# Other distances for the loads, splits, turns and swaps of q, k and v in a fused attention and feed-forward kernel

## The chip, the cores and the metric

The kernel runs on one core of a Trainium2 chip. The metric is the device time of one execution in microseconds (us), and lower is better. The engines are called by their short names: PE (TensorE, matmuls), ACT (ScalarE), DVE (VectorE), POOL (GpSimd) and SP (SyncE, which issues most of the DMAs here).

## The reference

Attention runs over 8 batches and 8 heads, with 576 rows of 64 numbers each for q, k and v. Scores under the row's maximum less tau (0.02) are cut off before the softmax. The heads are put side by side to rows of 512, and two matrix products with a shrinking function between them follow.

```python
scores = scale * np.matmul(q, k.transpose(0, 1, 3, 2))
thresh = np.max(scores, axis=-1, keepdims=True) - tau
scores = np.where(scores >= thresh, scores, -1000000000.0)
attn = np.exp(scores - np.max(scores, axis=-1, keepdims=True))
attn = attn / (np.sum(attn, axis=-1, keepdims=True) + 1e-09)
x = np.matmul(attn, v)            # then (b, h, s, d) -> (b * s, h * d)
h = x @ w_in                      # 4608 x 512 by 512 x 2048
out = (h - np.tanh(h)) @ w_out    # 2048 x 512
```

## The kernel before

**Pairs, tiles and slots.** Two heads of one batch make a pair; there are 32 pairs (`NPAIR`), four to a batch. A pair's scores are cut into nine tiles of 128 query rows by 576 keys: four for each head and a ninth of the 64 remaining rows of both. A main loop over `s` is the schedule, written out by hand (the tile framework runs in its manual order). One value of `s` is called a slot here, and one score tile belongs to each. In slot `s` the loop emits the scores of tile `s + 8` (`AHEAD`), the cut-off of tile `s + 5` (`MASK`), the exp of tile `s` and the product with v of a tile two slots back (`LAG`). Every engine's instructions stand in the order in which the loop emits them.

**One tile's way.** `scores(i)` runs the products on PE in fp16: q and k are each split into a high and a low half of fp16 which lie side by side on the 128 partitions, so the product with `kT` and the one with `kS` (k with its two halves swapped) are summed (L401 for the ninth tile, L410 for the others). DVE scales the tile and takes its maximum (L420). ACT applies the cut-off (`kink`, L447, writes z). For the first six pairs PE turns z; from pair 6 on SP issues a DMA transpose for every second tile, which takes two tiles at once (L454, zT from z). ACT then applies the exp (`weights`, L483, writes pT), and PE multiplies with v (`attend`, L506, L513, L524). That transpose is issued five slots ahead of the exp that reads it. Counted from the slot of a pair's first scores, these transposes lie at even distances (2, 4, 6, 8, 10) for an even pair, and zT(-10) stands for the one ten slots before that slot.

**Preparing a pair.** Six kinds of step make q, k and v ready. A load brings them from memory in up to two parts: `load_part` (L175) is issued by ACT's queue, and the steps are named `k0`, `q0`, `q1`, `v0` and `v1`. `split` (`ks`, `qs`: L228, L231, L232, three POOL instructions) makes the fp16 halves, khl or qhl. `turn` (`kt`, `qt`: L315) is a DMA transpose on SP's queue for q from pair 8 and for k from pair 9; before that PE turns them. `swap` (`kw`: L337, two POOL copies) makes kS from kT. `split_v` (`vs`: L261, L265, L266) casts v on POOL. The raw tiles and the halves have two buffers each, kT, kS and qT three, v four.

**Where these steps stand.** For pairs 8 and up the tables `LATER` (by even and odd pair) and `FIRST_LATER` (pairs 8 and 9) give each step a distance in slots. A step with distance `d` goes to the slot `9p - 8 - d`, which is `d` slots before the slot of the pair's first scores, and is emitted at the end of that slot, behind the scores, cut-offs, exps and products. So a step of distance 9 follows zT(-10) and precedes zT(-8) in SP's queue. [...]POOL's splits, casts and swaps of an even pair and of the odd pair after it are one queue, and SP's zT transposes, turns and stores of the output are another.

**The rest of PE's work.** Between the attention steps the loop emits the two products of the feed-forward part for an earlier batch: `hidden` (L579, psH), then tanh on ACT (`bend`, L592) and the difference on DVE (`shrink`, L598, writes g), then `project` (L605, psY). After the last attention tile these run alone.

Of the kernel before, what the change touches and what calls it, by code (L numbers as in the profile page):

```python
# [18 lines left out]
def kernel(  # L19
# [713 lines left out]
    def w_load(piece):  # L733
# [6 lines left out]
        else:  # L740
# [18 lines left out]

    LATER = {  # L760
        0: (
            ("kt", 11), ("qt", 7), ("k0", 18), ("q0", 17), ("v0", 13),
            ("q1", 14), ("v1", 10), ("ks", 12), ("qs", 8), ("vs", 4),
            ("kw", 6),
        ),
        1: (
            ("kt", 10), ("qt", 6), ("k0", 18), ("q0", 14), ("v0", 15),
            ("q1", 13), ("v1", 12), ("ks", 11), ("qs", 8), ("vs", 6),
            ("kw", 5),
        ),  # L770
    }
# [4 lines left out]
            ("kw", 3),  # L776
        ),
        9: (
            ("kt", 10), ("qt", 6), ("k0", 18), ("q0", 14), ("v0", 15),
            ("q1", 13), ("v1", 12), ("ks", 11), ("qs", 8), ("vs", 6),  # L780
            ("kw", 5),
        ),
    }
# [177 lines left out]
```

## Time and profile before

| what | us |
|---|---|
| median of 3 runs | 507.79 |
| lowest and highest run | 505.07, 510.07 |
| profiled execution, its own time | 511.62 |
| its span, first to last instruction | 509.7 |
| PE busy | 484.8 |
| ACT busy | 431.7 |
| DVE busy | 400.2 |
| POOL busy | 291.4 |

The profile is of one execution. Its span is 1.9 us less than that execution's own time, and this execution took 3.8 us more than the median of the runs. A row of the timeline has the start, the length, the engine (SPq and ACTq are the DMA issues of SP and ACT), the line of the kernel, the operation, and what is written from what (out<-in). A row of the waits has who waited for what, the sum in us, how many times, and the longest.

### The profile page before, as it was taken

What the parts mean: (1) busy time and instruction counts of PE and PEld (TensorE: products, weight loads), DVE (VectorE), ACT (ScalarE), POOL (GpSimd) and SP (SyncE); (2) the same over time, 40 slices, a digit from 0 to 9 for tenths busy, and PEclk for the clock granted to TensorE, in tenths of its full rate; (3) what the DMA queues carried; (4) which work ended last, traced back from release to release, by engine and by line L of the source; (5) the groups of instructions that cost most, each with busy time, mean ns of one, the idle gap of its engine ahead of it and who ended that gap; (6) DMA issues with size and microseconds to landing.
All of it is one profiled execution on the core that took longest, in us unless ns stands there. A gap on an engine that the chain in (4) does not pass through costs nothing.

```text
span 509.7 us, 12184 instructions
## 1 busy us (share of the span) xinstructions
PE 484.8 (95%) x4283; PEld 270.9 (53%) x4345; DVE 400.2 (79%) x1150; ACT 431.7 (85%) x617; POOL 291.4 (57%) x390
## 2 busy tenths in 40 slices
PE   8999899889999989999999999999998999999997
PEld 4666566445555545555555555555554555544444
DVE  5899978878889879988898789889886887544440
ACT  5999998889999889999999999899979999533430
POOL 8999999886765375757675666569456700000000
PEclk9999999989999999999999999999999999999999
DMA  7852658999999999999999999999999986311013
GB/s 206 262 155 89 195 190 220 159 225 214 231 217 245 192 254 209 238 241 242 242 195 221 261 238 225 207 242 240 213 191 258 187 144 115 87 41 42 23 41 82
DMA packets 233341, 95.32 MB, mean 187 GB/s; under 512 B 203968, under 2 KB 222656, under 8 KB 233280
## 3 DMA queue, kind: packets, MB, share of 16 engines
q1 hardware_dynamic: 212336, 72.87, 75.1%
q10 hardware_dynamic: 20944, 21.67, 16.1%
q8 instruction: 34, 0.56, 0.5%
q14 instruction: 27, 0.22, 0.2%
HBM read 36.70 MB, written 9.44 MB: 91 GB/s over the span
## 4 chain that ended last, share of the span: by engine, by line
PE 57%; POOL 12%; DMA 9%; issue 7%; ACT 7%; DVE 5%; ACTq 1%; SPq 0%; POOLq 0%; DVEq 0%
PE psY L605 18%; PE psH L579 14%; PE psS L410 13%; DMA zT<-z 6%; PE psO L513 3%; POOL kS L337 3%; PE psHt L579 3%; ACT pT L483 3%; DMA vraw<-in_v_dram 3%; ACT z L447 2%; DVE g L598 2%; POOL qhl L232 2%; DVE sc L420 2%; PE psS L401 2%; ACTq L175 1%
## 5 line engine op out<-in xcount | busy, mean ns | idle before, releaser
L420 DVE TENSOR_SCALAR_CACHE_REDUCE sc<-psS 128x576 f32<-128x576 f32 x288 | 213.5, 752 | 27.1 <-PE psS L410 12.9
L447 ACT ACTIVATE z<-sc,nb 128x576 bf16<-128x576 f32 x288 | 216.1, 770 | 8.0 <-DVE nb L432 5.7
L483 ACT ACTIVATE pT<-zT 128x1152 f16<-128x1152 bf16 x117 | 135.2, 1155 | 12.3 <-DMA zT<-z 10.6
L605 PE MATMUL psY<-w_out_sb,g 128*128 128x512 bf16 (+1 forms) x564 | 140.8, 373 | 1.6 <-issue 0.2
L579 PE MATMUL psH<-xT,w_in_sb 128*128 128x512 bf16 x448 | 119.4, 381 | 5.1 <-issue 2.0
L337 POOL COPY kS<-kT 64x1152 f16<-64x1152 f16 x62 | 70.8, 1142 | 86.3 <-DMA kT<-khl 72.7
L598 DVE SCALAR_TENSOR_TENSOR g<-th,psH 128x512 bf16<-128x512 f32 x128 | 87.6, 685 | 33.6 <-ACT th L592 32.9
L410 PE MATMUL psS<-kT,qT 128*128 128x512 f16 (+1 forms) x512 | 104.7, 286 | 4.1 <-DVE sc L420 1.9
L410 PE MATMUL psS<-kS,qT 128*128 128x512 f16 (+1 forms) x512 | 105.1, 287 | 0.0
L410 PEld LDWEIGHTS <-qT 128*128 128x128 f16 x1024 | 72.5, 98 | 59.0 <-issue 3.8
L592 ACT ACTIVATE th<-psH 128x512 f32<-128x512 f32 x128 | 74.6, 583 | 21.4 <-PE psH L579 21.4
L605 PEld LDWEIGHTS <-g 128*128 128x128 bf16 x592 | 51.1, 98 | 54.6 <-DVE g L598 0.4
L579 PEld LDWEIGHTS <-w_in_sb 128*128 128x128 bf16 x576 | 49.4, 98 | 57.4 <-issue 6.3
L513 PE MATMUL psO<-vb,pT 128*128 128x65 bf16 x1024 | 53.3, 194 | 0.0
L513 PEld LDWEIGHTS <-pT 128*128 128x128 f16 x1024 | 44.2, 98 | 9.6
L232 POOL TENSOR_TENSOR qhl<-qraw,qhl 128x576 f16<-128x576 f32 x31 | 39.7, 1281 | 2.6
L232 POOL TENSOR_TENSOR khl<-kraw,khl 128x576 f16<-128x576 f32 x31 | 39.7, 1280 | 2.7
L475 ACT ACTIVATE pT<-psZ 128x512 f16<-128x512 bf16 (+1 forms) x54 | 35.1, 654 | 2.4 <-PE psZ L466 2.1
L506 PE MATMUL psO<-vb,pT 128*128 128x130 bf16 x128 | 28.2, 220 | 3.7 <-ACT pT L483 3.6
L617 DVE COPY yo<-psY 128x512 f32<-128x512 f32 (+1 forms) x31 | 21.1, 680 | 13.1 <-PE psY L605 12.4
L539 DVE TENSOR_TENSOR osb<-psO,rc 128x256 bf16<-128x256 f32 x64 | 27.2, 424 | 2.2
L228 POOL TENSOR_SCALAR qraw<-qraw 128x576 f32<-128x576 f32 x31 | 20.8, 671 | 11.1 <-DMA qraw<-in_q_dram 10.8
(77 smaller groups left out, 452.1 us busy)
## 6 DMA issues: line engine op xcount, KB each, us to landing
out_dram<-yo SPq DMA_DIRECT2D x32, 256.0 KB, 3.8
kraw<-in_k_dram ACTq DMA_DIRECT2D x24, 288.0 KB, 4.2
qraw<-in_q_dram ACTq DMA_DIRECT2D x24, 256.0 KB, 4.3
wt<-in_moe_w_in_dram SPq DMA_DIRECT2D x8, 512.0 KB, 4.6
wt<-in_moe_w_out_dram SPq DMA_DIRECT2D x8, 512.0 KB, 3.9
vraw<-in_v_dram ACTq DMA_DIRECT2D x24, 160.0 KB, 4.3
vraw<-in_v_dram ACTq DMA_DIRECT2D x24, 128.0 KB, 3.8
vraw<-in_v_dram SPq DMA_DIRECT2D x8, 256.0 KB, 3.6
```

The lines of the kernel that those rows point to most:

```text
L232: nc.gpsimd.tensor_tensor(out=hl[:, :, 1, :], in0=x, in1=hl[:, :, 0, :], op=ALU.subtract)
L337: nc.gpsimd.tensor_copy(out=o, in_=i)
L410: nc.tensor.matmul(out=ps[:, dst], lhsT=lhs, rhs=cols(p, kk, hh), start=(n == 0), stop=(n == 1),)
L420: nc.vector.tensor_scalar(out=sc, in0=ps[:, lo : lo + S], scalar1=SC, scalar2=None, op0=ALU.mult, op1=ALU.max, accum_out=mx[:, c : c + 1],)
L447: nc.scalar.activation(out=z, in_=sc, func=ACT.Prelu, bias=nb, scale=1.0, alpha=STEEP)
L475: nc.scalar.activation(out=pt[:, off * P : (off + n) * P], in_=ps[:, 0 : n * P], func=ACT.Exp)
L483: nc.scalar.activation(out=pt[:, 0 : n * P], in_=zts.pop(i)[:, 0:n, :], func=ACT.Exp)
L513: nc.tensor.matmul(out=po[:, t - 1 + ab, :], lhsT=pt[:, blk * P : (blk + 1) * P], rhs=vb[:, hh, c, :], start=False, stop=(n == 7), skip_gr ...
L579: nc.tensor.matmul(out=ps, lhsT=w_in_sb[:, c, n * P : (n + 1) * P], rhs=xs[m][:, c, :] if m < B else xR[:, c, :, :], start=(c == 0), stop= ...
L592: nc.scalar.activation(out=th, in_=ps, func=ACT.Tanh)
L598: nc.vector.scalar_tensor_tensor(out=gs[m][:, n, :], in0=th, scalar=-1.0, in1=ps, op0=ALU.mult, op1=ALU.add,)
L605: nc.tensor.matmul(out=ps, lhsT=gs[m][:, n, ms * P : (ms + 1) * P], rhs=w_out_sb[:, n, cols], start=(n == 0), stop=(n == DF_C - 1),)
```

## The change

Only numbers in the two tables change, so the same instructions are emitted in another order on ACT's load queue, POOL and SP. For even pairs from 10: the turn of k goes from 11 slots before the scores to 9, the split of q from 8 to 10, the cast of v from 4 to 6, the swap of k from 6 to 3, the second part of q's load from 14 to 15 and that of v's from 10 to 12. For odd pairs from 9: the split of k goes from 11 to 14, the split of q from 8 to 9, the first load of k from 18 to 20, q's two parts from 14 and 13 to 15 and 14, and the first part of v from 15 to 16. Pair 8 keeps its own table. Two neighbours in POOL's queue change places: an even pair's swap of k now follows the next odd pair's split of k and that even pair's own cast of v.

```diff
     LATER = {
         0: (
-            ("kt", 11), ("qt", 7), ("k0", 18), ("q0", 17), ("v0", 13),
-            ("q1", 14), ("v1", 10), ("ks", 12), ("qs", 8), ("vs", 4),
-            ("kw", 6),
+            ("kt", 9), ("qt", 7), ("k0", 18), ("q0", 17), ("v0", 13),
+            ("q1", 15), ("v1", 12), ("ks", 12), ("qs", 10), ("vs", 6),
+            ("kw", 3),
         ),
         1: (
-            ("kt", 10), ("qt", 6), ("k0", 18), ("q0", 14), ("v0", 15),
-            ("q1", 13), ("v1", 12), ("ks", 11), ("qs", 8), ("vs", 6),
+            ("kt", 10), ("qt", 6), ("k0", 20), ("q0", 15), ("v0", 16),
+            ("q1", 14), ("v1", 12), ("ks", 14), ("qs", 9), ("vs", 6),
             ("kw", 5),
         ),
     }
...
         9: (
-            ("kt", 10), ("qt", 6), ("k0", 18), ("q0", 14), ("v0", 15),
-            ("q1", 13), ("v1", 12), ("ks", 11), ("qs", 8), ("vs", 6),
+            ("kt", 10), ("qt", 6), ("k0", 20), ("q0", 15), ("v0", 16),
+            ("q1", 14), ("v1", 12), ("ks", 14), ("qs", 9), ("vs", 6),
             ("kw", 5),
         ),
```

## The prediction, made before the result was known

> **What bounds the kernel now.** I read the stretches first. The six steps that the change moves belong to the pairs whose turns go by DMA, so only the time from 100 us to about 440 us counts; after that the projections run out alone. Columns: length, then busy time of PE, PEld, DVE, ACT and POOL with instruction counts, granted clock, DMA share, GB/s.
>
> ```profile
> 120.00:180.00 60.00, 59.32 (x533) 32.78 (x541) 52.51 (x157) 57.78 (x80) 37.09 (x47) 1.00 1.22 219
> 180.00:200.00 20.00, 18.50 (x155) 9.68 (x155) 15.31 (x46) 18.62 (x26) 14.89 (x20) 1.00 1.12 228
> 200.00:320.00 120.00, 118.49 (x1052) 65.20 (x1069) 106.65 (x315) 116.31 (x160) 78.25 (x100) 1.00 1.19 234
> 320.00:340.00 20.00, 19.14 (x177) 10.72 (x177) 16.48 (x52) 18.21 (x26) 10.24 (x13) 1.00 1.24 216
> 340.00:380.00 40.00, 39.58 (x344) 21.74 (x349) 35.73 (x105) 38.34 (x54) 25.79 (x36) 1.00 1.23 231
> 380.00:400.00 20.00, 17.80 (x157) 9.46 (x158) 15.19 (x46) 17.03 (x24) 13.13 (x17) 1.00 1.19 210
> 400.00:440.00 40.00, 39.00 (x331) 21.31 (x335) 30.92 (x88) 36.62 (x50) 6.00 (x8) 1.00 0.76 141
> ```
>
> PE is idle 20 us x 16 less 311.8 us busy, so 8.2 us in all from 120 to 440 us. [...]a 512-column matmul starts 215 to 216 ns after the one before it nearly everywhere, so the stretch is PE-bound and **8.2 us (1.6%) is all that a schedule can win here**. ACT is almost as full (about 96%). What the waits in the same stretch name:
>
> ```profile
> POOL kS L337 <- DMA kT<-khl: 71.0, 19, 7.9
> ACT pT L483 <- DMA zT<-z: 8.8, 10, 2.2
> ```
>
> POOL waits a lot in `swap` (L337) for the turned k, but POOL has room. ACT's 8.8 us are the waits that reach PE: the exp (L483) waits for its transposed scores, then PE waits for the exp. So what matters is when SP issues each zT transpose[...]. SP's own rows around an even pair's turn:
>
> ```profile
> 275.69 1.49 SPq L454 DMA_TRANSPOSE zT<-z  x1
> 277.67 2.71 SPq L315 DMA_TRANSPOSE kT<-khl  x1
> 280.47 3.42 SPq L454 DMA_TRANSPOSE zT<-z  x2
> 283.99 1.38 SPq L315 DMA_TRANSPOSE qT<-qhl  x1
> ```
>
> SP ends 275.69 + 1.49 = 277.18 and starts the turn at 277.67: 0.49 us idle. Between most neighbours it is 0.10 us, so 0.38 us was a wait. The z that the 280.47 row takes had ended at 277.80; the turn held it back.
>
> [...]a zT row lasts 1.47 us in the median and lands 4.7 us after its start.[...]
>
> **The change part by part.** A slot is one score tile; over the pairs it lasts 1.45 to 1.5 us (a pair of nine is 12.5 to 15 us). No instruction is added or removed.
>
> *Gap between split and turn* (even k 1 to 3 slots, q 1 to 3; odd k 1 to 4, q 2 to 3). What it can remove is SP waiting for POOL. From 110 to 425 us I took every hole before a turn of k over the usual 0.10 us whose end lies 28 ns after a split: 0.16 + 0.38 + 0.23 + 0.50 + 0.04 = **1.3 us over 22 pairs**; q's turn has none. POOL already runs ahead. Only the 0.38 us one reaches an ACT wait. I take 0.4 us of ACT; bounds 0 and 1.3.
>
> *Even turn of k from 11 to 9 slots before the scores.* zT transposes are issued at even distances here, so the turn leaves the place before zT(-10) and comes before zT(-8); q's turn stays at 7, before zT(-6). SP's order becomes zT, kT, zT, qT, zT, where one place of pause lay between. I moved the rows by hand for the even pairs 12 to 30, with each row's own length. zT(-10) is issued 0.2 to 2.6 us earlier; zT(-8) 0 to 1.1 us later; zT(-6) 0 to 0.7 us later, 0.35 us typically. What they have to spare, from landing to the exp that reads it (0.08 us means that the exp was started by it):
> - zT(-10): 0.08 five times of 11, and ACT waited 1.09 + 1.05 + 0.03 us there. Gain: up to 2.2 us of ACT; the 1.09 us is in a stretch where every DMA was slow (zT landings of 7 to 8.8 us from 167 to 177 us), so I take 1.3.
> - zT(-8): 0.08, 0.08, 0.15, 1.03, then more. A delay of 0.35 us costs 1.0 us in the sum over 12.
> - zT(-6): 0.08, 0.08, 0.14, 0.26, 0.42, 0.53, 0.72, 0.74, 0.77, then more. A delay of 0.35 us costs 1.2 us in the sum, 0.7 us costs 3.4, 1.5 us costs 10.6.
>
> So ACT: -0.4 - 1.3 + 1.0 + 1.2 = **+0.5 us**. PE lost 8.2 us while ACT waited 8.8, but about 2 us of PE's are 0.16 us holes after the remainder tiles (L401) of every two pairs, so 6 of 8.8: a factor of 0.7. That is +0.35 us.
>
> *Swap of k, even, from 6 to 3.* Both copies (2 x 1.14 us) are queued on POOL behind v's casts and behind the next odd pair's split of k (0.67 + 0.66 + 1.28 us), which was behind the swap before. Those have their data long before kT lands, so the swap still starts when kT lands. New turn start: zT(-10)'s issue end, about 12.2 us before the pair's first scores, plus a landing of 5.2 us median, 8.8 worst, plus 2.3 us of copies: done 4.7 us ahead in the median, 1.1 us in the worst. It is wanted about 0.7 us ahead (I count from the first score's row on DVE; its matmuls start that much sooner). Cost 0; if a slow DMA stretch meets it, 1 to 2 us once. Behind the swap stands the odd pair's split of q, wanted by SP some 8 us later: no cost.
>
> *Loads earlier* (odd k by 2 slots, q0, q1 and v0 by 1; even q1 by 1, v1 by 2). Same number of issues on ACT, each in a slot of its own. Splits already find their data except 10.8 us of POOL waits on q, which only shorten. The raw buffers are two deep and the split two pairs back is done over ten slots before: no wait for them on ACT. The 160 KB of v and 288 KB of k that stood beside zT(-10) and zT(-8) come two slots sooner, beside zT(-12), which has 1.6 us to spare in the median; v0 and q0 come one slot nearer to qT and zT(-6). The trace can't price this: between -1 and +2 us; I take 0.
>
> *v's casts, even, two slots earlier*: three POOL instructions (0.62 + 0.29 + 0.29 us), read by PE much later. Nothing.
>
> Sum: +0.35 us on the profiled execution, 511.62 us with 509.7 us of span. That execution lies 3.8 us above the median of 507.79, by the slow DMA stretches that account for its stalls at 183 and 382 us, which the change doesn't touch. Against the median: 508.1 us.
>
> **Rivals.**
> - *Faster*: the places before zT(-10) and after an odd turn lose their waits and the earlier loads keep clear of even turns. Of 8.2 us of idle PE, some 2 us are fixed; winning the other 6 gives 501.8, half of it 504.8. For it: ten zT waits, half of them next to turns. Against: the two largest are slow DMA stretches, not POOL.
> - *Slower*: the row of five transposes without a pause. Each holds SP 1.5 us, five need 7.3 us and have 8.8 us of slots; [...]zT(-6) comes 1.5 us late instead of 0.35. Price 10.6 us of ACT waits, times 0.7: +7.4 us, so 515. It decides from a mean delay of about 1.1 us (some 7 us of ACT, 5 us of PE). For it: zT(-6) has the least to spare now. Against: moved by hand, no pair exceeds 0.7 us.
> - *No effect at all*: SP never waited for the splits to begin with, 507.8.
>
> **How the numbers follow.** This kernel's runs spread from 505.07 to 510.07, so 1% (5.1 us) is what a measurement can tell from no change. No effect or nearly, with half a gain or a small loss on either side: 0.60, at 508.1, own range 505 to 511. Slower by over 1%: 0.28, since two tight places lie behind the new bunch, and the swap's cover shrinks from 6 to 3 slots. Faster by over 1%: 0.12, as it needs nearly all idle PE. The range goes to 502.5 and 515.
>
> **What would show it.** Right: zT(-10) issued within 0.5 us of its z in even pairs, spare time there up by a microsecond, zT(-6) down by some 0.3 us; holes before turns of k all 0.10 us; POOL's wait before swaps smaller or the same; idle PE from 120 to 440 us within 6 to 10 us. Wrong: PE rows waiting for kS at the first tile of even pairs (swap too late), ACT waits on zT over 15 us in the sum, or loads that land later than 5 us in the median.

## The result and the profile after

The changed kernel is slower: 513.34 us in the median of 15 runs, 508.38 us for the kernel before in as many, and a ratio of 1.0116 with a 95% interval of 1.009 to 1.0143. Every ratio here is of the fast runs alone (it leaves out runs over 1.5% above the fastest of their kernel), while the medians are over all runs, so a ratio can differ by some tenths of a percent from the quotient of the two medians. The time lies inside the range given (502.5 to 515), 5.2 us above the time forecast (508.1), and the ratio is on the slower side of the 1% line, which had been given 0.28. The profiled execution of after took 519.0 us (span 517.2), the longest of its 15, that of before 511.62 us; so the two traces differ by 7.4 us where the medians differ by 5.0, and sizes read from them are on the large side.

The stretches of after, with the columns as in the prediction (length, then busy PE, PEld, DVE, ACT and POOL with counts, granted clock, DMA share, GB/s; the DMA share adds up the packets' own times, and reaches 1.23 here):

```profile
120.00:180.00 60.00, 56.78 (x502) 31.11 (x510) 49.58 (x150) 54.92 (x76) 37.14 (x47) 1.00 1.23 220
180.00:200.00 20.00, 18.95 (x167) 10.25 (x167) 15.93 (x48) 18.29 (x25) 11.18 (x14) 1.00 1.14 219
200.00:320.00 120.00, 115.79 (x1009) 62.96 (x1025) 101.75 (x301) 111.48 (x153) 75.55 (x97) 0.99 1.23 222
320.00:340.00 20.00, 16.50 (x129) 8.32 (x131) 13.08 (x41) 15.27 (x21) 8.93 (x12) 0.92 1.22 177
340.00:380.00 40.00, 38.65 (x343) 21.21 (x346) 34.48 (x101) 37.87 (x53) 25.95 (x34) 1.00 1.19 231
380.00:400.00 20.00, 19.74 (x182) 11.03 (x184) 17.47 (x53) 19.24 (x27) 15.06 (x21) 1.00 1.20 242
400.00:440.00 40.00, 39.23 (x327) 21.12 (x332) 32.74 (x95) 37.64 (x52) 8.24 (x10) 1.00 0.84 153
```

PE is idle for 320 - 305.6 = 14.4 us there, 8.2 us before. Idle time is not the whole loss in this trace: the granted clock was 0.51 from 234.2 to 237.6 us and from 336.6 to 340.0 us (the 0.92 of the stretch from 320 to 340). Each drop stands close to the end of a wait of PE for the exp, of 2.0 us to 233.2 and of 2.8 us to 336.7. Four matmuls of `project` take 1.90 us in the second and 1.03 at full clock, so each drop costs about 1.7 us (an estimate: half of 3.4). In the trace of before there is one such drop (0.50) ahead of the end, at 104.3 us, outside the stretch. That the waits caused the drops is not shown. The waits of the same stretch of after (who, for what, sum in us, times, longest):

```profile
POOL kS L337 <- DMA kT<-khl: 64.9, 20, 9.8
POOL qraw L228 <- DMA qraw<-in_q_dram: 24.9, 12, 4.3
ACT pT L483 <- DMA zT<-z: 19.6, 19, 3.3
PE psO L506 <- ACT pT L483: 6.5, 4, 2.8
```

ACT's waits for zT went from 8.8 us in 10 to 19.6 us in 19. This is the row that moved with the time: in the 14 profiles of this document it goes from 6.4 us (an execution of 506.36 us) to 20.1 us (518.97 us), and the five executions of over 516 us are the five with over 15 us of it. It moves with the time of the execution that was profiled, though, and not only with the kernel, so a row of one execution can't say by itself which kernel is slow; the ratios do that. POOL's longer waits for q (24.9 us, 10.8 before) and its shorter ones for kT (64.9 us, 71.0 before) don't reach PE: it has no wait for qT or kS in this stretch of after.

### The profile page after: what moved, and what is told of

It is laid out like the page before. It is cut to its first block, busy times and chain, and to the rows that moved or that the text cites. A ratio compares the mean times of both kernels' runs of the same rounds, so it can differ in the third digit from the quotient of the medians.

```text
span 517.2 us, 12173 instructions
## 1 busy us (share of the span) xinstructions
PE 487.9 (94%) x4283; PEld 271.7 (53%) x4345; DVE 399.6 (77%) x1150; ACT 432.4 (84%) x617; POOL 291.7 (56%) x390
## 4 chain that ended last, share of the span: by engine, by line
PE 56%; DMA 11%; ACT 9%; POOL 9%; issue 6%; DVE 6%; ACTq 1%; SPq 0%; POOLq 0%; DVEq 0%
PE psY L605 18%; PE psH L579 14%; PE psS L410 12%; DMA zT<-z 9%; ACT z L447 3%; PE psO L513 3%; ACT pT L483 3%; PE psHt L579 3%; POOL kS L337 2%; PE psS L401 2%; DVE g L598 2%; DVE sc L420 2%; DMA vraw<-in_v_dram 2%; ACT th L592 2%; ACTq L175 1%
## 5 line engine op out<-in xcount | busy, mean ns | idle before, releaser
L483 ACT ACTIVATE pT<-zT 128x1152 f16<-128x1152 bf16 x117 | 135.2, 1156 | 20.3 <-DMA zT<-z 19.6
L605 PE MATMUL psY<-w_out_sb,g 128*128 128x512 bf16 (+1 forms) x564 | 142.3, 376 | 1.6 <-issue 0.2
L337 POOL COPY kS<-kT 64x1152 f16<-64x1152 f16 x62 | 70.9, 1143 | 69.0 <-DMA kT<-khl 64.9
L228 POOL TENSOR_SCALAR qraw<-qraw 128x576 f32<-128x576 f32 x31 | 20.9, 673 | 24.9 <-DMA qraw<-in_q_dram 24.9
```

The source lines that it names most:

```text
L337: nc.gpsimd.tensor_copy(out=o, in_=i)
L483: nc.scalar.activation(out=pt[:, 0 : n * P], in_=zts.pop(i)[:, 0:n, :], func=ACT.Exp)
L605: nc.tensor.matmul(out=ps, lhsT=gs[m][:, n, ms * P : (ms + 1) * P], rhs=w_out_sb[:, n, cols], start=(n == 0), stop=(n == DF_C - 1),)
```

## The experiments

Each kernel differs from the kernel before, or from the changed one, only in distances of the two tables. The ratio is to the kernel before on the same chip, with its 95% interval. Three theories stood at the start. A: the turn of k, now in a row of transposes without a pause, makes the transposes late. B: the earlier loads do it through the DMA engines. C: the new order on POOL does it.

**The turn of k alone.**

```diff
 LATER[0]
-            ("kt", 11),
+            ("kt", 9),
```

> The kernel before with one edit: the even pairs' turn of k at 9 slots before the scores, not 11. Theory A (the turn of k sits in a row of five transposes without a pause, and the transposes behind it come late): 3 to 5 us slower than before, ratio 1.006 to 1.010. Theory B (the earlier loads press on the DMA engines where the transposes have least to spare): within 1 us of before. Theory C (the new order on POOL costs): within 1 us of before.

Measured: 507.95 us, ratio 1.0004 (0.9979 to 1.003). A, in the form of the prediction's slower rival, falls: the turn in its new place costs nothing that can be measured. From the waits of this kernel between 120 and 440 us, in an execution of 506.36 us (reader, what it waits for, sum in us, times, longest):

```profile
ACT pT L483 <- DMA zT<-z: 6.4, 8, 1.7
```

**The loads alone.**

```diff
 LATER[0]
-            ("q1", 14), ("v1", 10)
+            ("q1", 15), ("v1", 12)
 LATER[1], FIRST_LATER[9]
-            ("k0", 18), ("q0", 14), ("v0", 15), ("q1", 13)
+            ("k0", 20), ("q0", 15), ("v0", 16), ("q1", 14)
```

> The kernel before with only the load distances of the change (even q1 15, v1 12; odd k0 20, q0 15, v0 16, q1 14). Theory B: 3 to 5 us slower than before, ratio 1.006 to 1.010. Theories A and C: within 1 us of before.

Measured: 514.49 us, ratio 1.0112 (1.0074 to 1.015). This is as large as the change's whole effect, as theory B says, and a little over the 1.010 that it gave. The same row of this kernel's waits, in an execution of 518.97 us, is as long as that of after:

```profile
ACT pT L483 <- DMA zT<-z: 20.1, 15, 3.4
```

**The change with the old turn of k.**

```diff
 the changed kernel, LATER[0]
-            ("kt", 9),
+            ("kt", 11),
```

> The changed kernel with the even turn of k put back to 11 slots. Theory A: back to the kernel before within 1.5 us. Theories B and C: as slow as the changed kernel, 4 to 6 us over before.

Measured: 517.6 us, ratio 1.0191 (1.014 to 1.0243), on six runs. Putting the turn back doesn't help. The kernel is some 9 us over before, more than the 4 to 6 us that B and C gave: with the earlier loads the old place of the turn is, on these few runs, worse than the new one. No theory had that, and it stays unexplained.

**The change with the old loads.**

```diff
 the changed kernel, LATER[0]
-            ("q1", 15), ("v1", 12)
+            ("q1", 14), ("v1", 10)
 LATER[1], FIRST_LATER[9]
-            ("k0", 20), ("q0", 15), ("v0", 16), ("q1", 14)
+            ("k0", 18), ("q0", 14), ("v0", 15), ("q1", 13)
```

> The changed kernel with all load distances put back. Theory B: back to the kernel before within 1.5 us. Theories A and C: as slow as the changed kernel, 4 to 6 us over before.

Measured: 507.56 us, ratio 0.999 (0.996 to 1.0021). So the splits, casts, swaps and the turn of k together are worth nothing that can be measured with the old loads, and C falls too. The row in this kernel (an execution of 506.08 us) is that of before again:

```profile
ACT pT L483 <- DMA zT<-z: 8.4, 10, 2.0
```

**Which load?** B was divided: into a run of three loads in adjacent slots (v0 and v1 of the even pair, k0 of the odd one, after the change), k0 by itself, and the loads that moved by one slot.

```diff
 k0_20, LATER[1], FIRST_LATER[9]
-            ("k0", 18),
+            ("k0", 20),
 v1_12, LATER[0]
-            ("v1", 10),
+            ("v1", 12),
 oneslot, LATER[0]
-            ("q1", 14),
+            ("q1", 15),
 oneslot, LATER[1], FIRST_LATER[9]
-            ("q0", 14), ("v0", 15), ("q1", 13),
+            ("q0", 15), ("v0", 16), ("q1", 14),
 after_k0v1_back: the changed kernel with
-            ("k0", 20), and for even pairs ("v1", 12)
+            ("k0", 18), and for even pairs ("v1", 10)
```

> The kernel before with one edit: the odd pairs' load of k at 20 slots, not 18. Theory B1 (three loads of v, v and k in adjacent slots press on the transposes; needs both this move and that of v's second part): within 2.5 us of before. Theory B2 (the 288 KB of k alone, now ahead of the even pair's tight transposes, costs it all): 4 to 6 us slower, ratio 1.008 to 1.012. Theory B3 (the loads moved by one slot, of q and v, cost): within 1 us of before.

> The kernel before with one edit: the even pairs' second part of v at 12 slots, not 10, so that it stands in the slot behind v's first part. Theory B1: within 2.5 us of before. Theories B2 and B3: within 1 us of before.

> The kernel before with only the loads that the change moves by one slot (even q1 15; odd q0 15, v0 16, q1 14). Theory B3: 4 to 6 us slower, ratio 1.008 to 1.012. Theories B1 and B2: within 1 us of before.

> The changed kernel with two distances put back: the odd pairs' load of k at 18, the even pairs' second part of v at 10. Theories B1 and B2: back to the kernel before within 1.5 us. Theory B3: as slow as the changed kernel, 4 to 6 us over before.

Measured: k0 alone 1.0108, but from 1.0005 to 1.021 on six runs that spread from 505.6 to 522.3 us; v1 alone 1.0 (0.9968 to 1.0032); the one-slot moves 1.009 (1.0059 to 1.012); the change with k0 and v1 put back 1.0114 (1.0049 to 1.0179) on six runs. The run of three is not it: the change stays as slow without it. The moves by a single slot, which I had held for the harmless ones, are enough for most of it. The row in the kernel with the one-slot moves only, in an execution of 517.76 us, the longest of its 22:

```profile
ACT pT L483 <- DMA zT<-z: 17.4, 16, 2.6
```

**One load at a time.**

```diff
 q0_15, LATER[1], FIRST_LATER[9]
-            ("q0", 14),
+            ("q0", 15),
 v0_16, LATER[1], FIRST_LATER[9]
-            ("v0", 15),
+            ("v0", 16),
 k0_20_again: as k0_20
 later: the changed kernel, even pairs
-            ("q1", 15), ("v1", 12)
+            ("q1", 14), ("v1", 10)
 later, odd pairs
-            ("k0", 20), ("q0", 15), ("v0", 16), ("q1", 14)
+            ("k0", 18), ("q0", 13), ("v0", 14), ("q1", 12)
```

> The kernel before with one edit: the odd pairs' first load of q (256 KB) at 15 slots, not 14, so that it is issued one slot behind the even pair's turn of q and not two. Theory D1 (this load on top of that turn makes the transposes late): most of the 0.9% of the four one-slot moves together, ratio 1.005 to 1.009. Theory D2 (the first part of v, which now comes between that turn and the transpose before it): within 1 us of before. Theory D3 (only the sum of the one-slot moves costs): 1.002 to 1.004.

> The kernel before with one edit: the odd pairs' first part of v (128 KB) at 16 slots, not 15. Theory D2: ratio 1.005 to 1.009. Theory D1: within 1 us of before. Theory D3: 1.002 to 1.004.

> The changed kernel with the loads of before, and the odd pairs' q and first part of v moved one slot the other way (q0 13, v0 14, q1 12, and 18 for k). If the loads cost by how near they come to the even pair's turn of q: 1 to 3 us under the kernel before, ratio 0.994 to 0.998. If each place is as good as the next and only that of the change is bad: within 1 us of before. If any move off the places of before costs: 3 to 5 us slower.

> The same kernel as the one with only the odd pairs' load of k at 20 slots, whose interval was too wide. If that load costs by itself: ratio 1.006 to 1.013. If the first look was chance: within 1 us of before.

Measured: q0 alone 512.35 us, **ratio 1.0099 (1.0061 to 1.0137)**; v0 alone 1.002 (0.9991 to 1.0049); k0 again 1.0034 (1.0 to 1.0068); the odd loads one slot later than before 1.0027 (0.9998 to 1.0055). One number, the odd pairs' 256 KB load of q from 14 to 15, is as slow as the four one-slot moves and nearly as slow as the change. The ratio is that of theory D1, at a little more than it gave. The edit moves a second load in time: at 15 q0 stands in one slot with v0 and ahead of it on ACT's queue, so that v0 is issued 0.3 us ahead of the even pair's turn of q in the median, not 2.1. In the other kernels with q0 at 15 v0 keeps its place (1.4 to 2.0 us ahead) and they are as slow, so the move of v0 isn't needed for the loss.

The load of k is less settled. Its second measurement, 1.0034, falls between what was expected of a real cost and of chance. By the medians of all runs k0 alone is 0.6% over before (511.47 to 508.45 us) and q0 alone 0.8% (512.35), and these two can't be told apart; so what k0 costs by itself is open, from nothing to most of what q0 costs. The change doesn't need it: with k0 and v1 put back it is as slow. Nor did the kernel with the odd loads later do what any of its three expectations said. It isn't faster than before, so the distance of the load from the turn of q alone doesn't set the time.

Taken together: the six kernels with q0 at 15 have ratios from 1.009 to 1.0191, with no interval that reaches under 1.0049; those with q0 at 14 or 13 lie between 0.999 and 1.0034, but for the first six runs of k0.

**What that load meets.** SP's rows and ACT's load around one even pair's turn of q, in the kernel before (rows of SP, then of ACT; x2 is two issues in one row, of which the start is that of the first, here of q0):

```profile
228.55 1.61 SPq L454 DMA_TRANSPOSE zT<-z  x1
230.26 1.26 SPq L315 DMA_TRANSPOSE qT<-qhl  x1
```

```profile
231.33 1.02 ACTq L175 DMA_DIRECT2D qraw<-in_q_dram  x2
```

and in the kernel with q0 alone moved, around the same pair's turn:

```profile
222.81 4.64 SPq L454 DMA_TRANSPOSE zT<-z  x2
227.55 1.30 SPq L315 DMA_TRANSPOSE qT<-qhl  x1
```

```profile
226.15 0.39 ACTq L175 DMA_DIRECT2D qraw<-in_q_dram  x1
```

Before, the load is issued 1.07 us behind the turn of q, and in the other kernel 1.40 us ahead of it, though its slot is still the one behind the turn's. Over the eleven even pairs from 10 to 30 (start of the odd pair's load less start of the even pair's turn, median; landing time from issue, mean):

| kernel | load less turn, us | zT before the turn lands in | turn of q lands in | ratio |
|---|---|---|---|---|
| before | +1.09 | 5.03 | 4.59 | 1 |
| turn of k alone | +0.75 | 4.97 | 5.13 | 1.0004 |
| change, old loads | +0.92 | 4.98 | 4.82 | 0.999 |
| v1 alone | +1.72 | 5.59 | 4.95 | 1.0 |
| v0 alone | +1.61 | 5.07 | 4.97 | 1.002 |
| odd loads later | +1.65 | 4.32 | 5.04 | 1.0027 |
| k0 alone | +1.40 | 4.57 | 5.00 | 1.0108 |
| k0 alone, again | +1.41 | 4.92 | 5.00 | 1.0034 |
| q0 alone | -2.25 | 5.53 | 5.62 | 1.0099 |
| one-slot moves | -1.33 | 6.36 | 5.61 | 1.009 |
| loads alone | -0.71 | 5.66 | 5.62 | 1.0112 |
| after | -1.11 | 5.73 | 5.67 | 1.0116 |
| change, old turn of k | -0.78 | 5.73 | 5.62 | 1.0191 |
| change, k0 and v1 back | -1.08 | 5.85 | 5.87 | 1.0114 |

In every kernel with q0 at 15 the load stands ahead of the turn in the median; then the turn of q lands after 5.6 to 5.9 us instead of 4.6 to 5.1, and this holds in the short profiled executions too (q0 alone, 509.5 us; k0 and v1 put back, 508.82 us). The zT before it, zT(-8), lands after 5.5 to 6.4 us instead of 4.3 to 5.6; here v1 alone is a counterexample, with a zT as late as q0's (5.59 us) and no loss. The exp that reads zT(-8) lost its spare time in after: 0.08 us in the median (six of 11 at 0.08 us), 1.70 us before.

Late landings are shown, then, but not that the loss of time goes through these two transposes. By place (slots before the even pair's scores are negative), ACT's waits for zT rose from before to after by 2.6 us at zT(-8), 3.2 at zT(-12), 2.2 at zT(-2), 2.3 at zT(0), 2.1 at zT(4) and 0.5 at zT(-6), and fell by 2.1 at zT(-10): 10.8 us in the sum, of which zT(-8) is a quarter. That the issue of the load takes ACT's own time is not the cause: no idle time of ACT in after or in the q0 kernel is put down to an issue.

Where the load is later than before, the waits move on: in the kernel with the odd loads later, zT(-6) has 0.08 us to spare in the median and ACT waits 10.1 us there, none in before. With k0 alone moved (second measurement) zT(-12) has 0.08 us to spare, 1.6 us before, and ACT waits 7.1 us there, 0.2 before. In the kernel with all the loads, where k0 is moved as well, 9.8 of the 20.1 us lie at zT(-12), so k0 does show there. A reading of this, not tested further, is that each load has some transpose beside it, and that the places of before are those where the transposes hit had most to spare.

**What stays open.** The profiled execution of the q0 kernel took 509.5 us, the shortest of its 13 (median 512.35), and shows only 6.5 us of ACT waits for zT, 0.2 of them at zT(-8). The kernel with the odd loads later, whose profiled execution was the longest of its 22 (519.11 us, median 510.39), shows 15.7 at a ratio of 1.0027. The rows of q0 alone and of the odd loads later:

```profile
ACT pT L483 <- DMA zT<-z: 6.5, 12, 1.3
```

```profile
ACT pT L483 <- DMA zT<-z: 15.7, 13, 2.7
```

So the runs show that q0's move costs time, and the traces show that the turn behind it lands late. The way from there to idle PE isn't shown: the long rows of waits come from long executions, and which transposes carry the loss of the q0 kernel stays open. Why one slot (about 1.45 us) moved the load by 1.8 to 3.3 us against the turn wasn't tried; where it was 3.3, q0 had also passed v0. That it is the load that delays the transposes is my inference from the landing times, not isolated: no run left the load out, and by which way it would delay them isn't shown. None of the kernels measured here beats the kernel before; the turn of k alone, v1 alone and the change with the old loads are equal to it.

## Why the prediction was right or wrong

- **What bounds the kernel: right.** PE's idle time and ACT's waits for zT are what changed between the two profiled executions, by 6.2 us and 10.8 us, a factor of 0.57 where 0.7 was taken. The drops of the clock, which no line of the prediction had, come on top. ACT's "about 96%" was 95% (302.9 of 320 us).
- **Gap between split and turn: right, and worth as little as said.** After the change the holes on SP before turns of k are 0.10 to 0.13 us, but for 0.17 at the first three, as before. The change with old loads has all these gaps and stands at 0.999.
- **The turn of k from 11 to 9: right in size and place**, as far as one execution of each kernel can tell. With the turn alone, ACT waits at zT(-10) went from 2.1 us to 0, at zT(-8) from 1.3 to 2.6, at zT(-6) from 0 to 2.0. The sum, +1.2 us, was put at +0.9 without the gap's share. In after zT(-10) was issued within 0.03 us of its z in the median and its spare time rose from 0.41 to 2.12 us; that of zT(-6) didn't fall (0.52 to 0.87 us). The run of transposes without a pause, the slower rival, didn't act; its delay of 1.5 us was an estimate, from SP's long zT rows (2.4 us at the ninth decile before).
- **The swap from 6 to 3: right.** In after the even swaps end 5.2 us ahead of the scores in the median and 3.1 in the worst case (4.7 and 1.1 were put); PE never waits for one. POOL kept the order of the tables on which this rested: in both traces the 80 splits, casts and swaps of the pairs from 12 on start in it.
- **Loads earlier: wrong, and this is the step that failed.** It said that v0 and q0 "come one slot nearer to qT and zT(-6)", bounded it by -1 and +2 us, and took 0. The loads alone cost 1.12%, 5.7 us on 508.4, and q0 alone 0.99%. The move was read in slots and not in time: q0 stood 1.1 us behind the turn of q, so one slot didn't only bring it nearer, it carried it across, and the transposes that land later are the turn itself and zT(-8). zT(-6), which the prediction named, kept its spare time in after. How the late landings become 5 us of the kernel's time stays open. The upper bound had no reason from a row; the trace of before did hold a hint, had I sorted its transposes by the loads near them. From 120 to 420 us the 30 zT with under 150 KB issued within 2.5 us on either side land after 4.55 us in the mean and the 64 with 150 to 450 KB after 5.19, though the 6 with over 450 KB land after 4.70; of the turns of k ten have 150 to 450 KB (5.58 us) and ten over 450 KB (6.13 us).
- **"Which only shorten" on POOL's waits for q: wrong, without effect.** They rose from 10.8 to 24.9 us. With the loads alone they fell to 6.4, so it is the earlier split of q that waits; POOL has the room (busy 182 of the 320 us in after).
- **The signs of being wrong.** ACT waits on zT of over 15 us were named, and came (19.6 us); idle PE left the 6 to 10 us of the right case (14.4 us). Both are of a long execution. Loads that land later than 5 us in the median didn't come: from 120 to 440 us all loads went from 4.18 to 4.48 us, the 256 KB ones from 4.16 to 4.97.
- **The chances.** No effect had 0.60 and the answer came from the 0.28. Both reasons given for that 0.28 (two tight places behind the bunch, and the swap's cover) didn't act, and the term that decided had been set to 0. That the time lies in the range is luck: the range goes up to 515 because of the slower rival, and the loss came from elsewhere.

## What to carry to other kernels

Here moving a load on one queue so that it passed a transpose on another cost 1% (1.0099 with q0 alone). So where loads and transposes are issued on several queues, treat the order in time between the queues as part of the schedule: before moving a load by a slot, find in the trace which transfers of the other queue it now passes, and what those have to spare until their reader. A bound for such a move has to come from rows, for instance landing times of one kind of transfer sorted by the bytes issued near them, and not from the smallness of the move. A stall that a table names on the issuing engine should be looked for as a hole between its rows before work goes into removing it: from 110 to 425 us of before the table of SP's waits puts 37.0 us at the turns (L315) down to POOL, the holes that ended at a split came to 1.3 us, and the change with the old loads, which has the wider gaps, stands at 0.999. And a table of waits from one execution describes that execution: compare kernels by many runs first, and only then by traces.

## What the runs showed of the hardware

The zT transposes (128 by 1152 two-byte numbers) hold SP for 1.24 us at least and land after 3.2 us at least, 4.7 us in the median in the kernel before and 10.1 us at worst in after. What I hadn't expected is how much the place of a single 256 KB load on another queue is worth: with q0 alone moved, 2.25 us ahead of the turn in the median, two transposes for each two pairs land 0.5 and 1.0 us later in the mean, and the kernel takes 1% longer, while a move of 160 KB by two slots elsewhere (v1) didn't change the time.
